# Weight tiles in pairs, and another form of the key and value loads, in a kernel of two attentions and two MoE layers on one core

## Chip, core and metric

One core of a Trainium2 chip. The metric is device time in microseconds (us) of one execution of the whole program, the median of several runs. Lower is better. The engines are named as the profile names them: PE (TensorE matmul; PEld its weight load), DVE (VectorE), ACT (ScalarE), POOL (GpSimd) and SP (SyncE, which issues all DMAs here).

## What is computed

The inputs q, k and v are float32 of shape (2, 8, 576, 64): two batches, eight heads, 576 tokens. The weights of the two layers come in float64.

```python
q_d, k_d, v_d = means of q, k, v over groups of 4 tokens   # 144 rows
out_up    = repeat(softmax(q_d @ k_d.T / 8) @ v_d, 4)
out_local = softmax(where(|i - j| < 4, q @ k.T / 8, -1e9)) @ v
x = out_up + out_local          # seen as 1152 tokens x 512

h = x @ w_in                    # 512 -> 2048
g = (a0 + a1*h + a2*h*h + a3*h*h*h) / (1 + |b0|*|h| + |b1|*h*h + 1e-6)
x = g @ w_out                   # 2048 -> 512

h = x @ w_in2
out = (h * tanh(softplus(h))) @ w_out2
```

## The kernel before

**Planner.** The kernel is first written as some thousand tasks (`add`, line 79), each with the engines that may run it and an estimated duration, a priority (a due time in us), the tasks it waits for, and the buffers it takes or uses. `Plan.run` (line 105) then plays the program through with these durations and writes every engine's instructions in the order in which they start there. The order within an engine is fixed from then on; on the chip an instruction waits on semaphores for what it needs, and all that stand behind it on its engine wait too. Where PE would idle for too long in the first part, `fill` (line 147) writes matmuls whose result nobody reads (lines 445 and 448), which keep its clock up; these are called fillers here.

**Attention.** Four pairs of heads in each of two batches are worked in 24 units (`unit`, line 532) of up to four windows of 64 queries. `prep` (line 469) does once per pair what its units share: it loads two heads of k with one DMA (96 partitions, six tokens of two heads in each, so pieces of 64 words), turns them round with six PE transposes (line 467), copies them into kT in two passes of 288 words (line 492), sums groups of four (line 500), and loads v for the down-sampled attention with one DMA over 72 partitions (line 509) that lines 518 and 522 sum. A unit loads its queries (line 546) and two windows of v (line 558), makes the scores (lines 612 to 623), the softmax (ACT line 640, DVE lines 633 to 666, POOL line 660), transposes (678, 682), the two products with v (713, 719), and writes x as two float32 parts, xh and xl (749, 754).

**MoE.** All products are made in three matmuls from a high and a low part of each operand. The 2048 columns of a layer are taken in groups (6, 6 and 4 tiles of 128 in the first layer, four times 4 in the second), and in each group the tokens in chunks: 256, 256, 256 and 384 in the first group of the first layer, else three times 384. A step is two tiles of one chunk: h by line 974, the rational function (ACT 995, 1000, 1003; DVE 1010, 1013, 1018 and others) or Mish (1068), its high and low part, and the second product by line 1122 or 1124. Steps with 384 tokens use buffers and banks of the attention, so they wait for its end (`att_done`, line 825), and so do the weights of all groups but the first (`gate`, line 842).

**Weights.** Each of the 64 weight tiles of 128 x 512 words comes as 64-bit words by one DMA into one of four raw buffers (line 848 for w_in, 853 for w_out) and is made into two float32 parts without 64-bit arithmetic: ACT scales the upper words (859) and shifts the lower ones (865), DVE joins them (872) and sets the sign (878), ACT or DVE writes the high part (884, 886), DVE the low part (889). Four buffers `wt` hold what is between; the parts go to rings of six tiles for each of w_in and w_out, after attention of nine.

```python
raw_t = [const.tile([128, DM], w_in1.dtype, name=f"raw{i}") for i in range(NRAW)]
wt_t = [const.tile([128, DM], F32, name=f"wt{i}") for i in range(NWT)]
x = add({"sp": 1.45}, load, pr - LLEAD, take=[r], chain="wld")
y = add({"act": 0.52}, scale, c, after=[x], take=[t], use=[r], chain="wsc")
z = add({"act": 0.52}, low, c, after=[x], use=[r])
x = add({"dve": t_dve(DM)}, join, c, after=[y, z], use=[t, r], port=True)
x = add({"dve": t_dve(DM)}, sign, c, after=[x], use=[t, r], port=True)
```

**What sets the order.** A step's due time is the PE time of all steps before it. Attention units of a chunk are due LEAD before it, the load of a weight tile LLEAD and its conversion CLEAD before its first step, w_out tiles OLAG after w_in; VOFF, VROFF, LOFF and KOFF shift the loads of attention (lines 26 to 36).

## Time and profile before

| what | value |
|---|---|
| median of 3 runs | 522.7 us (521.2 to 527.63) |
| the profiled execution | 523.05 us, of which its span 521.3 us |
| granted TensorE clock, mean | 0.993 |
| PE busy | 500.3 us, 96% of the span, 3530 matmuls |
| DVE busy | 378.4 us, 73%, 648 instructions |
| ACT busy | 356.1 us, 68%, 734 instructions |
| POOL busy | 74.2 us, 14%, 102 instructions |
| DMA | 46.54 MB, mean 89 GB/s, 56764 packets, 32784 of them under 512 B |

The span runs from the first instruction to the last. Busy time counts an engine's instructions, fillers as well; a busy PE is not PE at its peak. The shares are averages over stages with different limits.

### The profile page before, as it was taken

Reading aid. Unit: us, or ns where it says so; the run is one execution under the profiler, and the core shown is the slowest. Engines: PE = TensorE matmul, PEld = TensorE weight load, DVE = VectorE, ACT = ScalarE, POOL = GpSimd, SP = SyncE. Lnnn points to the kernel's source line nnn. Section 1 sums busy time; section 2 is a strip of 40 time slices with the busy share of each in tenths; the row PEclk is TensorE's granted clock in tenths of the full one; section 3 lists DMA queues with packets and bytes.
Section 4 is the critical chain, followed back from the end, with each engine's and each line's share of the span. In section 5 each row is a group of like instructions: output and inputs, shape, how many; then the busy total and the mean of one; then the engine's idle time right before and its main releaser. Section 6 shows DMA issues by size and latency. Waiting matters only on the chain.

```text
span 521.3 us, 9187 instructions
## 1 busy us (share of the span) xinstructions
PE 500.3 (96%) x3530; PEld 450.5 (86%) x3530; DVE 378.4 (73%) x648; ACT 356.1 (68%) x734; POOL 74.2 (14%) x102
## 2 busy tenths in 40 slices
PE   9889998988999999999799999999999999999997
PEld 5567676877999999999799989989998999889995
DVE  4777889898999999988999999998732632231322
ACT  4588788898788899998999998789821521112210
POOL 3553564234100000000000033400000000000000
PEclk9998999999999999999999999999999999999999
DMA  9979655432132114311340222467600000000111
GB/s 160 192 182 190 118 124 142 128 94 60 43 123 79 41 41 121 123 53 70 121 162 3 98 63 80 123 189 236 219 2 0 1 1 1 0 1 0 62 60 62
DMA packets 56764, 46.54 MB, mean 89 GB/s; under 512 B 32784, under 2 KB 51472, under 8 KB 56720
## 3 DMA queue, kind: packets, MB, share of 16 engines
q1 hardware_dynamic: 56720, 45.95, 33.2%
q8 instruction: 28, 0.46, 0.4%
q14 instruction: 16, 0.13, 0.1%
HBM read 43.58 MB, written 2.36 MB: 88 GB/s over the span
## 4 chain that ended last, share of the span: by engine, by line
PE 50%; ACT 20%; DVE 16%; DMA 8%; issue 3%; SPq 2%; POOL 0%; ACTq 0%; DVEq 0%
PE psum L974 22%; PE psum L1124 19%; PE psum L1122 5%; DMA raw<-in_moe_w_in_dram 3%; DMA raw<-in_moe_w_out_dram 2%; ACT wt L859 2%; ACT raw L865 2%; ACT wrk L1000 2%; ACT att L640 1%; ACT late_f L1003 1%; DMA wrk<-in_v_dram 1%; DVE part L1167 1%; ACT late_f L995 1%; ACT gg L1089 1%; DVE wt L878 1%
## 5 line engine op out<-in xcount | busy, mean ns | idle before, releaser
L974 PE MATMUL psum<-xh,wi 128*128 128x384 f32 (+1 forms) x600 | 153.4, 326 | 1.5 <-DVE wrk L1018 0.8
L974 PEld LDWEIGHTS psum<-xh,wi 128*128 128x128 f32 x600 | 107.1, 188 | 3.9 <-DVE wrk L1018 1.2
L974 PE MATMUL psum<-xl,wi 128*128 128x384 f32 (+1 forms) x300 | 96.5, 322 | 0.0
L1122 PE MATMUL psum<-gg,wo 128*128 128x256 f32 (+1 forms) x432 | 68.4, 311 | 1.3 <-DVE gg L1094 0.4
L1122 PEld LDWEIGHTS psum<-gg,wo 128*128 128x128 f32 x432 | 64.5, 189 | 3.4 <-DVE wo L889 0.8
L974 PE MATMUL psum<-xh,late_r 128*128 128x384 f32 x216 | 57.6, 335 | 0.7 <-DVE late_f L1018 0.7
L974 PEld LDWEIGHTS psum<-xl,wi 128*128 128x128 f32 x300 | 56.5, 188 | 0.3
L859 ACT ACTIVATE wt<-raw 128x512 f32<-128x512 f32 x64 | 43.0, 674 | 9.2 <-DVE wrk L1013 2.3
L1124 PE MATMUL psum<-wo,gg 128*128 128x512 f32 x207 | 48.8, 390 | 0.0
L872 DVE SCALAR_TENSOR_TENSOR wt<-wt,raw 128x512 int32<-128x512 int32 x64 | 44.8, 716 | 4.4 <-ACT raw L865 2.4
L1124 PEld LDWEIGHTS psum<-wo,gg 128*128 128x128 f32 x207 | 38.8, 188 | 7.9
L878 DVE SCALAR_TENSOR_TENSOR wt<-raw,wt 128x512 int32<-128x512 int32 x64 | 45.0, 711 | 0.2
L865 ACT ACTIVATE raw<-raw 128x512 int32<-128x512 uint16 x64 | 42.9, 676 | 2.8 <-DMA raw<-in_moe_w_out_dram 1.9
L1068 ACT ACTIVATE wrk<-psum 128x768 f32<-128x768 f32 (+1 forms) x13 | 10.2, 787 | 48.5 <-PE psum L974 48.5
L1201 DVE TENSOR_TENSOR part<-psum,part 128x512 f32<-128x512 f32 x27 | 18.2, 691 | 34.3 <-PE psum L1124 34.3
L1181 POOL TENSOR_TENSOR xl<-part,xh 128x768 fp32r<-128x768 f32 x6 | 14.3, 2396 | 184.3 <-DVE xh L1178 175.1
L974 PEld LDWEIGHTS psum<-xh,late_r 128*128 128x128 f32 x216 | 39.3, 188 | 1.2 <-PE psum L974 1.0
L1068 ACT ACTIVATE late_f<-psum 128x768 f32<-128x768 f32 (+1 forms) x12 | 9.4, 782 | 40.1 <-PE psum L974 40.1
L974 PE MATMUL psum<-xl,late_r 128*128 128x384 f32 x108 | 36.2, 336 | 0.0
L1094 DVE TENSOR_TENSOR gg<-wrk,gg 128x768 fp32r<-128x768 f32 (+2 forms) x23 | 19.4, 849 | 20.9 <-ACT gg L1068 20.8
L1094 DVE TENSOR_TENSOR gg<-late_f,gg 128x768 fp32r<-128x768 f32 x14 | 13.4, 956 | 18.9 <-ACT gg L1068 18.3
L448 PE MATMUL psum<-mask,ident 128*128 128x480 bf16 x89 | 24.0, 375 | 0.1
(133 smaller groups left out, 1010.1 us busy)
## 6 DMA issues: line engine op xcount, KB each, us to landing
raw<-in_moe_w_in_dram SPq DMA_DIRECT2D x32, 512.0 KB, 4.1
raw<-in_moe_w_out_dram SPq DMA_DIRECT2D x32, 512.0 KB, 6.3
out_dram<-part SPq DMA_DIRECT2D x9, 256.0 KB, 2.0
att<-in_v_dram SPq DMA_DIRECT2D x32, 60.0 KB, 4.3
att<-in_k_dram SPq DMA_DIRECT2D x6, 288.0 KB
att<-in_v_dram SPq DMA_DIRECT2D x6, 288.0 KB
att<-in_q_dram SPq DMA_DIRECT2D x16, 96.0 KB, 4.5
att<-in_v_dram SPq DMA_DIRECT2D x8, 80.0 KB, 7.9
```

The costliest lines, as they stand in the source:

```text
L448: nc.tensor.matmul(view[:, :6 * WK], ident16, mask[:, :6].rearrange("p w x -> p (w x)"), start=True, stop=True)
L859: nc.scalar.activation(out=t.v, in_=words(r)[:, :, 1].bitcast(F32), func=AF.Identity, scale=2.0 ** -112)
L865: nc.scalar.activation(out=words(r)[:, :, 0], in_=r.v.bitcast(U16).rearrange("p (n four) -> p n four", four=4)[:, :, 1], func=AF.Copy, sca ...
L872: nc.vector.scalar_tensor_tensor(out=ti, in0=ti, scalar=3, in1=words(r)[:, :, 0], op0=ALU.logical_shift_left, op1=ALU.bitwise_or)
L878: nc.vector.scalar_tensor_tensor(out=ti, in0=words(r)[:, :, 1], scalar=SIGN, in1=ti, op0=ALU.bitwise_and, op1=ALU.bitwise_or)
L974: nc.tensor.matmul(st.h.v[:, i, :T], w.v[:, ww, ks], xx[:, kk, c0:c0 + T], start=(nn == 0 and (st.big or i == 0)), stop=(nn == 3 * KD - 1 ...
L1068: nc.scalar.activation(out=vw(dst), in_=H(), func=AF.Mish)
L1094: ENG[e].tensor_tensor(out=vw(st.gl), in0=vw(st.c), in1=vw(st.gh).bitcast(F32), op=ALU.subtract)
L1122: nc.tensor.matmul(A(d)[:, :T], w.v[:, ww, sl], vw(gg)[:, i, :], start=start, stop=stop)
L1124: nc.tensor.matmul(A(d), vw(gg)[:, i, sl], w.v[:, ww, :], start=start, stop=stop)
L1181: ENG[e].tensor_tensor(out=xl[xs], in0=pv, in1=xh[xs].bitcast(F32), op=ALU.subtract)
L1201: nc.vector.tensor_tensor(out=pv, in0=acc.v[:, j], in1=pv, op=ALU.add)
```

## The change

Weight tiles are loaded and converted two at a time: a DMA of 128 x 1024 64-bit words, six passes of 1024 words instead of twice six of 512. Raw and `wt` buffers are two of double size instead of four, the rings three pairs for each kind, after attention five pairs for w_in and four for w_out. A step takes its half of a pair. In `prep`, the four pairs of heads that come first load each head's six tokens as one piece of 384 words, so a transpose holds two tokens of one head, and the copy to kT is four passes over 64 partitions instead of two over 128. The load of v is two DMAs, over 64 and over 8 partitions. Five numbers of the planner change, and some of its estimated durations.

```diff
-LEAD, CLEAD, LLEAD, OLAG = 30, 2, 35, 13
-PROL, PSTEP, VOFF, VROFF, LOFF, KOFF = -45, 1.5, 5, 0, 11, 12
+LEAD, CLEAD, LLEAD, OLAG = 25, 5, 35, 10
+PROL, PSTEP, VOFF, VROFF, LOFF, KOFF = -45, 1.5, 0, 0, 11, 12
...
-NRAW, NWT, NRING, NRING2 = 4, 4, 6, 3
+NRAW, NWT, NRING, NRING2 = 2, 2, 3, (2, 1)
...
-    raw_t = [const.tile([128, DM], w_in1.dtype, name=f"raw{i}") for i in range(NRAW)]
+    raw_t = [const.tile([128, 2 * DM], w_in1.dtype, name=f"raw{i}") for i in range(NRAW)]
...
+            if start:
+                nc.sync.dma_start(
+                    out=kn.v.rearrange("p (h x) -> p h x", h=2), in_=src.rearrange("h (p r) d -> p h (r d)", r=6)
+                )
...
+            if start:
+                for e2 in range(2):
+                    copies.append((
+                        lambda src=src, e2=e2: src()[64 * e2:64 * e2 + 64],
+                        lambda g=g, e2=e2: kT[p][64 * g:64 * g + 64].rearrange("c (p r e) -> c p r e", r=3, e=2)[:, :, :, e2],
+                        t, pt,
+                    ))
...
+            src = v[bb, 2 * p:2 * p + 2].rearrange("h (t p f) d -> p (h t) (f d)", t=2, f=4)
+            dst = vr.v.rearrange("p x f d -> p x (f d)")
+            for lo, hi in ((0, 64), (64, 72)):
+                nc.sync.dma_start(out=dst[lo:hi], in_=src[lo:hi])
...
-                    in_=src[:, f * 128:(f + 1) * 128].rearrange("(k p) f -> p k f", p=128),
+                    in_=src[:, f * 256:(f + 1) * 256].rearrange("(k p) f -> p k f", p=128),
...
-                nc.sync.dma_start(out=r.v, in_=(w_out1, w_out2)[m][f * 128:(f + 1) * 128, :])
+                nc.sync.dma_start(
+                    out=r.v.rearrange("p (a d) -> p a d", a=2),
+                    in_=(w_out1, w_out2)[m][f * 256:(f + 1) * 256, :].rearrange("(a p) d -> p a d", p=128),
+                )
...
-            y = add({"act": 0.52}, scale, c, after=[x], take=[t], use=[r], chain="wsc")
-            z = add({"act": 0.52}, low, c, after=[x], use=[r])
-            x = add({"dve": t_dve(DM)}, join, c, after=[y, z], use=[t, r], port=True)
+            y = add({"act": 1.04}, scale, c, after=[x], take=[t], use=[r], chain="wsc")
+            z = add({"act": 1.04}, low, c, after=[x], use=[r])
+            x = add({"dve": t_dve(2 * DM)}, join, c, after=[y, z], use=[t, r], port=True)
...
-                w, wd = W[m, "i", f]
+                w, wd = W[m, "i", f // 2]
```

The lines of the changed kernel that answer to those above: fillers 445 and 448 as before; key loads 475 (start) and 479, key copies 508 and 510, v load 530, windows of v 576, queries 564; weight loads 866 and 871, weight passes 880, 886, 893, 899, 905, 907 and 910; h product 996, second product 1144 and 1146; last attention product 737.

Three places in the order of the engines' instructions. First SP, at the start, from the fourth key load on (`in_k`, `in_q`, `in_v` are the inputs, `att` and `wrk` the memory that receives them). Before:

```order
L474 DMA wrk<-in_k_dram 96x12x64
L546 DMA att<-in_q_dram 128x4x64
L509 DMA att<-in_v_dram 72x4x256
L509 DMA wrk<-in_v_dram 72x4x256 x2
L546 DMA att<-in_q_dram 96x4x64
L558 DMA att<-in_v_dram 80x4x64 x2
L546 DMA att<-in_q_dram 64x4x64
L558 DMA att<-in_v_dram 80x4x64 x2
L509 DMA att<-in_v_dram 72x4x256
L546 DMA att<-in_q_dram 96x4x64
L558 DMA att<-in_v_dram 80x4x64 x2
L848 DMA raw_71<-in_moe_w_in_dram 128x4x128
```

Now, from the first load of v on:

```order
L530 DMA att<-in_v_dram 64x4x256
L530 DMA att<-in_v_dram 8x4x256
L576 DMA att<-in_v_dram 80x4x64 x2
L530 DMA wrk<-in_v_dram 64x4x256
L530 DMA wrk<-in_v_dram 8x4x256
L576 DMA att<-in_v_dram 80x4x64 x2
L530 DMA wrk<-in_v_dram 64x4x256
L530 DMA wrk<-in_v_dram 8x4x256
L530 DMA att<-in_v_dram 64x4x256
L530 DMA att<-in_v_dram 8x4x256
L564 DMA att<-in_q_dram 96x4x64
L866 DMA raw_71<-in_moe_w_in_dram 128x4x256
```

The loads of v and the first windows of v now stand ahead of the fifth query load, and one weight load of double size takes the place of the first two. Second ACT, where the first weight tiles are converted among the softmax passes (640, now 658) of attention. Before:

```order
L640 ACTIVATE att<-psum,att 128x80 x4
L644 ACTIVATE att<-psum,att 128x144
L859 ACTIVATE wt_75<-raw_71 128x512
L699 ACTIVATE att<-psum 80x512
L865 ACTIVATE raw_71<-raw_71 128x512
L859 ACTIVATE wt_76<-raw_72 128x512
L865 ACTIVATE raw_72<-raw_72 128x512
L731 ACTIVATE att<-psum 128x64
L640 ACTIVATE att<-psum,att 128x80 x3
```

Now:

```order
L605 ACTIVATE att<-psum 128x192
L880 ACTIVATE wt_73<-raw_71 128x1024
L658 ACTIVATE att<-psum,att 128x80 x4
L662 ACTIVATE att<-psum,att 128x144
L749 ACTIVATE att<-psum 128x64
L717 ACTIVATE att<-psum 80x512
L439 ACTIVATE b_sb<-b_sb 128x2
L605 ACTIVATE att<-psum 128x128
L767 ACTIVATE xh<-att 128x256
L886 ACTIVATE raw_71<-raw_71 128x1024
```

Four passes of 512 words have become two of 1024; the first of them now stands ahead of the softmax passes of a unit with four windows (658 x4), where before such passes stood ahead of it. Third PE at the last attention product (lines 713 and 719, now 731 and 737; `wi` and `wo` are weight tiles, `mask` with 480 columns a filler). Before:

```order
L448 LDWEIGHTS ident_62
L448 MATMUL psum<-mask,ident_62 128x480
L974 MATMUL psum<-xh,wi_79 128x256
L974 MATMUL psum<-xl,wi_79 128x256
L974 MATMUL psum<-xh,wi_79 128x256
L974 MATMUL psum<-xh,wi_80 128x256
L974 MATMUL psum<-xl,wi_80 128x256
L974 MATMUL psum<-xh,wi_80 128x256
L713 MATMUL psum<-att 64x48 x4
L719 MATMUL psum<-att 64x64 x6
L1122 MATMUL psum<-gg,wo_90 128x256 x12
L974 MATMUL psum<-xh,wi_79 128x256
```

Now:

```order
L1144 MATMUL psum<-gg,wo_80 128x256 x24
L696 MATMUL psum<-ident,att 72x128 x2
L700 MATMUL psum<-ident,att 80x128 x3
L996 MATMUL psum<-xh,wi_76 128x256
...
L731 MATMUL psum<-att 64x48 x4
L737 MATMUL psum<-att 64x64 x6
L996 MATMUL psum<-xh,wi_76 128x256
...
L1144 MATMUL psum<-gg,wo_78 128x256 x24
L996 MATMUL psum<-xh,wi_75 128x384
```

Fillers stand close to the last product before and not now; the MoE work on both sides of it is another part of the first group, and the first product of 384 columns comes sooner after it.

## Rows read from the trace of the kernel before

**Rows 1.** Busy time of each engine by stretches (us), granted clock, DMA share

```profile
core 0: us, PE busy (x) PEld busy (x) DVE busy (x) ACT busy (x) POOL busy (x), PEclk, DMA share, GB/s
0.00:140.00 140.00, 127.53 (x1489) 97.87 (x1490) 113.76 (x294) 110.62 (x386) 59.92 (x96) 0.99 0.63 134
140.00:310.00 170.00, 165.91 (x989) 163.48 (x987) 160.78 (x214) 156.88 (x213) 4.25 (x2) 0.99 0.27 84
310.00:521.00 211.00, 206.83 (x1055) 189.12 (x1054) 103.89 (x142) 88.58 (x136) 10.00 (x4) 1.00 0.20 64
...
100.00:120.00 20.00, 18.21 (x207) 15.14 (x206) 19.24 (x44) 19.40 (x58) 6.25 (x10) 1.00 0.34 99
```

**Rows 2.** Groups by form: fillers on PE; count, busy us, mean ns, idle before

```profile
L448 PE MATMUL psum<-mask,ident 128*128 128x480 bf16 x89 | 24.0, 375 | 0.1
L445 PE MATMUL psum<-part 128*128 128x480 bf16 x9 | 3.8, 604 | 1.2 <-DVE part L452 1.2
```

**Rows 3.** DMA queue from 0 to 20 us, then from 20 to 40 us

```profile
q1 hardware_dynamic: 9826, 3.19, 101.6%
...
q1 hardware_dynamic: 6889, 3.88, 79.0%
```

**Rows 4.** Timeline, waits for DMAs at the start: DVE, ACT, POOL

```profile
16.43 0.69 DVE L518 TENSOR_TENSOR wrk<-wrk 72x512 f32<-72x512 f32 x1 [0.78 <-DMA wrk<-in_v_dram]
...
27.29 0.68 ACT L859 ACTIVATE wt<-raw 128x512 f32<-128x512 f32 x1 [0.92 <-DMA raw<-in_moe_w_in_dram]
...
24.64 1.26 POOL L518 TENSOR_TENSOR att<-att 72x512 f32<-72x512 f32 x1 [3.80 <-DMA att<-in_v_dram]
```

**Rows 5.** Groups by form: a weight pass and MoE passes of two sizes

```profile
L872 DVE SCALAR_TENSOR_TENSOR wt<-wt,raw 128x512 int32<-128x512 int32 x64 | 44.8, 716 | 4.4 <-ACT raw L865 2.4 <-ACT wt L859 1.8
...
L1010 DVE TENSOR_TENSOR wrk<-wrk,psum 128x768 f32<-128x768 f32 x8 | 7.6, 952 | 3.4 <-ACT late_f L1003 1.6 <-ACT wrk L1000 1.5 <-ACT wrk L1003 0.3
L1013 DVE SCALAR_TENSOR_TENSOR wrk<-wrk,b_sb 128x512 f32<-128x512 f32 x9 | 7.1, 790 | 0.0
L1010 DVE TENSOR_TENSOR wrk<-wrk,psum 128x512 f32<-128x512 f32 x9 | 6.1, 682 | 1.4 <-ACT wrk L1003 1.3 <-ACT wrk L1000 0.2
...
L1000 ACT ACTIVATE wrk<-psum 128x768 f32<-128x768 f32 x18 | 14.5, 805 | 1.1 <-DVE wrk L1018 1.1
L1000 ACT ACTIVATE wrk<-psum 128x512 f32<-128x512 f32 x9 | 5.3, 593 | 0.0
```

**Rows 6.** Chain that ended last: start us, us, what

```profile
96.05 1.42 PE psum L974 x12
...
230.15 1.20 DVE wt L872 x2
```

**Rows 7.** Timeline of ACT: two weight passes in a row

```profile
41.94 0.68 ACT L859 ACTIVATE wt<-raw 128x512 f32<-128x512 f32 x1
42.50 0.67 ACT L865 ACTIVATE raw<-raw 128x512 int32<-128x512 uint16 x1
```

**Rows 8.** Timeline of PE at the fifth query flip, and fillers

```profile
18.60 0.36 PE L467 MATMUL psum<-ident,att 96*128 96x96 f32 x2 [0.86 <-DVE att L666]
18.79 0.97 PE L448 MATMUL psum<-mask,ident 128*128 128x480 bf16 x4
```

**Rows 9.** Timeline of ACT: two key copies of the start

```profile
9.41 0.80 ACT L492 ACTIVATE att<-psum 128x288 f32<-128x288 f32 x2 [2.03 <-PE psum L467]
```

**Rows 10.** Timeline of SP: the issue of the fifth query load

```profile
10.28 0.62 SPq L546 DMA_DIRECT2D att<-in_q_dram  x1
```

**Rows 11.** Timeline of PE: last attention product; both products of a 384-column step

```profile
132.53 0.53 PE L719 MATMUL psum<-att 80*64 80x64 f32 x12
...
160.27 0.34 PE L974 MATMUL psum<-xh,wi 128*128 128x384 f32 x1
...
176.72 4.32 PE L1122 MATMUL psum<-late_r,wo 128*128 128x384 f32 x24
```

More of the change, by code (lines that the diff above doesn't have):

```diff
@@ L473, in load @@
             src = k[bb, 2 * p:2 * p + 2]
-            nc.sync.dma_start(
-                out=kn.v.rearrange("p (r h d) -> p r h d", h=2, d=D),
-                in_=src.rearrange("h (p r) d -> p r h d", r=6),
-            )
-        ld = add({"sp": 1.6}, load, prio - KOFF, take=[kn], chain="ld")
+            if start:
+                nc.sync.dma_start(
+                    out=kn.v.rearrange("p (h x) -> p h x", h=2), in_=src.rearrange("h (p r) d -> p h (r d)", r=6)
+                )
+            else:
+                nc.sync.dma_start(
+                    out=kn.v.rearrange("p (r h d) -> p r h d", h=2, d=D),
+                    in_=src.rearrange("h (p r) d -> p r h d", r=6),
+                )
+        ld = add({"sp": 0.9 if start else 1.6}, load, prio - KOFF, take=[kn], chain="ld")
         copies = []
@@ L549, in qload @@
             )
-        l0 = add({"sp": 0.7}, qload, prio - LOFF, take=[qn], chain="ld")
+        l0 = add({"sp": 0.18 * nw}, qload, prio - LOFF, take=[qn], chain="ld")
         s0, step, m0 = window(w0, nw)
@@ L839 @@
         gate = []
-        if not (m == 0 and f < GROUPS[0][0]):
+        if not (m == 0 and 2 * f < GROUPS[0][0]):
             w.slots = ring_s[kind] + ring2[kind]
@@ L889, in lo @@
             ENG[e].tensor_tensor(out=w.v[:, 1], in0=s.v, in1=w.v[:, 0].bitcast(F32), op=ALU.subtract)
-        x = add({"sp": 1.45}, load, pr - LLEAD, take=[r], chain="wld")
+        x = add({"sp": 2.9}, load, pr - LLEAD, take=[r], chain="wld")
         src = r
```

55 lines of the change are left out of this document (29 added, 26 removed).

## Prediction

> **What bounds the kernel now.** I read the busy table by stretches first [rows 1]. Its TensorE (PE) column is the room that is left: from 310 us on PE is busy 206.8 of 211 us at full clock, from 140 to 310 it is busy 165.9 of 170. These 381 us are PE work and can give back little: 4.1 us idle in the middle, and some 1.7 us for a granted clock of 0.99 there (170 x 0.01). The first 140 us are another matter. PE is "busy" for 127.5 us, but the groups by form [rows 2] show that 3.8 + 24.0 = 27.8 us of it are 9 + 89 matmuls of lines 445 and 448, the fillers that the planner sets where it expects PE to idle. With 12.5 us of plain idle PE loses 40 us of these 140, while VectorE (DVE) is busy for 113.8 and ScalarE (ACT) for 110.6 us. So the change has to earn its time before 140 us, where attention, MoE steps and weight conversion share ACT and DVE. Last I read the DMA rows of the first 40 us, 16 engines taken by 101.6% and 79% [rows 3], and who waited for a DMA there [rows 4].
>
> **The passes.** In the order of instructions DVE has 205 weight passes before (64 x 3 and 13 casts) and 107 now; ACT has 179 before and 85 now. A merged pass saves its fixed part. DVE takes 952 ns for 768 words and 682 for 512 [rows 5]: 1.05 ns a word, 0.54 us for 512. Two passes of 512 back to back take 1.20 us in the chain [rows 6], 0.60 each, so 0.06 is fixed. ACT takes 805 and 593 ns [rows 5]: 0.83 ns a word, 0.43 us for 512. A pass of line 865 starts 0.56 us after one of line 859 [rows 7], so 0.13 is fixed. In all that is 98 x 0.06 = 5.9 us of DVE and 94 x 0.13 = 12.2 us of ACT, spread over the 64 tiles; it reaches the end only where PE waits for them.
>
> The Trainium skill, page "Perfetto Trace Analysis", section "Optimizing Scalar/DVE Operations", gives about 60 ns of overhead for a DVE and 93 ns for a ScalarE instruction on SBUF. The trace agrees for DVE and shows more for ACT; by the page ACT would save 94 x 0.093 = 8.7 us, an estimate.
>
> **What is moved ahead of the last attention step.** I count the order of both programs up to the last attention product (line 719 before, 737 now). Ahead of it stand 98 fillers before and 82 now, and 150 + 60 MoE matmuls of 256 columns before and 186 + 144 now. The 120 more are 120 x 1.42/12 [rows 6] = 14.2 us of PE work done earlier. DVE pays for it: up to the last attention add it has 14 more MoE passes (48 for 34) of some 0.74 us, the middle of 0.68 and 0.79 [rows 5], = 10.4 us; its weight passes go from 37 x 0.72 = 26.6 to 22 x (0.72 + 0.54) = 27.7 us. If DVE paces attention, attention ends 11.5 us later with 14.2 us more done: a gain of 2.7. If ACT paces it: 13 more MoE passes x 0.59 = 7.7, weight passes from 42 x 0.68 = 28.6 to 23 x (0.68 + 0.43) = 25.5, 8 more key copies at 0.40 (two take 0.80 [rows 9]) = 3.2; that is 7.8 us more, a gain of 6.4. By fillers: 16 fewer, between 0.20 us each where they follow one another (four in 0.97 us, the last shown with its whole 0.375 [rows 2, 8]) and 27.8/98 = 0.28: 3.2 to 4.5. I take 2.9, between DVE and the fillers at their pace, since DVE is as busy as ACT or busier; the ends are 2.7 and 6.4.
>
> **The start.** Four key loads go from 1152 pieces of 256 B each to 192 of 1536 B: 3840 packets fewer for the same bytes. From 0 to 20 us a packet of 325 B costs 1.016 x 16 x 20 us/9826 = 33 ns, from 20 to 40 us one of 563 B costs 37 [rows 3]. Along that line 256 B cost 32 and 1536 B 51 ns, and the engines are free (4608 x 32 - 768 x 51)/16 = 6.8 us earlier; if bytes alone set the price, it is 0. What waits for DMAs now: DVE 0.78 us for a value load, ACT 0.92 for a weight tile, POOL 3.80 for a value load [rows 4]. DVE's and ACT's, 1.7 us, lie on the path; with half of POOL's it is 3.6, with all of it 5.5, the upper end. Against it stand the 8 key copies on ACT (3.2 us), of which the 2.03 us that ACT idles beside them [rows 9] hide most, and on SP the fifth query load, now behind 12 value DMAs instead of 3. Nine issues of about 0.62 us put it at 10.28 + 5.6 = 15.9 us [rows 10]; its flip ran at 18.60, after a wait for DVE [rows 8], so a load that takes over 2.7 us to land is late on PE. One wait is added: on ACT the first weight pass (line 880) now stands ahead of the fourth unit's softmax, before (859) it stood behind it and still waited at 27.29 [rows 4]. Its load, of double size, follows the query load on SP, at some 16.5 us; if it lands 8 us later, the softmax and all that ACT does for the next units stand behind a wait of up to 3.5 us. I take a gain of 1.5; the ends are 5.5 and a loss of 3.2 + 3.5 = 6.7.
>
> **The middle.** PE's 5.8 us of idle and slow clock between 140 and 310 lie behind ACT and DVE, both busy for over 92% there [rows 1]. With some per cent less load I take half of it, 2.9, between 0 and 5.8. Against it: the first step of 384 columns now has 48 matmuls of 384 at 4.32/24 and 48 of 256 between its own two products, 8.6 + 5.7 = 14.3 us; before, 16.3 us lay between them (160.4 to 176.7 [rows 11]) with ACT and DVE full. 2.0 us may be missing; the net is 0.9. The two raw buffers of double size and the rings of 10 and 8 tiles (9 and 9 before) I cost at nothing: 16 tiles are issued by the end of attention in both orders, and the last pair of the second group's output weights has over 20 us of PE work between the release of its buffer and its use. If that cover goes, the three DVE passes of a pair (3 x 1.14 us) show once a group. Two of the six 768-word differences on POOL go to DVE at the switch to the second MoE, 2 x 0.95 us beside PE's own work.
>
> The sum is 2.9 + 1.5 + 0.9 = 5.3 us. The profiled execution took 523.05 us (span 521.3), 0.35 above the median of 522.7; it becomes 517.75, the median 517.4.
>
> **The rivals.** (A) It is hidden: the DMA waits of the start turn into waits for the key copies, the later query load and line 880, and DVE takes the lead of 14.2 us back. For it: by count 11.5 of the 14.2 are taken back already. Against it: 16 fillers fewer. Time 522.7, within 2. (B) ACT paces attention and the start gives all it has: 6.4 + 5.5 + 2.9 - 2.0 = 12.8, time 509.9. For it: ACT at 19.4 of 20 us from 100 to 120 us; against it DVE at 19.2 in the same row [rows 1]. (C) The cover is missing. The MoE work now done before attention ends is what PE lived on after it, while the first 384-column step went through ACT and DVE and while the second group's weights, which wait for attention to end, were converted. Before, 222 matmuls of 256 columns were left after the last attention product, 26.3 us; now it is 102, 12.1 us, against a latency of 16.3. If the whole lead is given back as idle there, the time is 517.4 + 14.2 = 531.6; slower than before from 5.3 us of new idle on. (D) Long passes block: a step behind a weight pass waits up to 1.14 instead of 0.60 us on DVE and 0.99 instead of 0.56 on ACT. There are 192 of these passes; each puts on average half the difference, 0.24 us, on what stands behind it. If one in four of these waits reaches PE, that is 192 x 0.24/4 = 11.5 us, time 528.9; it decides from about one in nine. For it: ACT and DVE have gaps in attention, where single steps wait for each other; against it: from 140 us on PE rarely waits at all.
>
> The same section of the Trainium skill says that where these engines are not saturated but cause bubbles elsewhere, breaking instructions up may let work finish sooner, the rule behind (D). The trace shows them saturated from 100 us on and not in the first 60.
>
> **How the numbers follow.** The forecast (513 to 521) has 0.43, A 0.18, B 0.19, C 0.11, D 0.09. Two per cent, about what a measurement of this kernel can tell from no change, is 512.2 to 533.2. Faster than that is B and a little of the forecast, 0.21; slower the upper parts of C and D, 0.07; within it 0.72. The range of 508 to 530 leaves out the far ends of B, C and D.
>
> **What would show it.** Right: passes near 1.2 us on DVE and 1.1 on ACT in the groups; fillers and idle of PE together under 36 us up to 140; the last attention product near 142 us (132.5 [rows 11] + 14.2 - 2.9 - 1.5), between 138 and 148; PE idle from there to 310 under 8 us. Wrong: over 6 us of PE idle in one place after attention (C); PE or ACT waiting often behind lines 893, 899 or 880 (D); ACT waiting over 2 us before line 880, or late with the key copies (A); attention's end before 138 (B).

## The result, and the profile after

| | before | after |
|---|---|---|
| median of 20 runs | 524.41 us (521.2 to 531.16) | 519.12 us (515.97 to 522.71) |
| ratio, 95% interval | | 0.9907 (0.9882 to 0.9932) |
| the profiled execution | 523.05 us, span 521.3 | 521.48 us, span 519.7 |
| granted TensorE clock in it, mean | 0.993 | 0.993 |

The change takes 0.93% off, 4.9 us of 524.41 by the ratio, and the interval lies wholly below 1. The forecast was 1.0%, 5.3 us, and 517.4 us lies 1.7 us below the median. Read the two profiles with care: they differ by only 1.6 us, because the profiled execution of before lies 1.4 us below the median of its kernel and that of after 2.4 us above.

First the busy time of after by stretches, to be laid beside [rows 1].

```profile
core 0: us, PE busy (x) PEld busy (x) DVE busy (x) ACT busy (x) POOL busy (x), PEclk, DMA share, GB/s
0.00:140.00 140.00, 124.77 (x1472) 97.62 (x1473) 114.00 (x273) 110.86 (x367) 60.75 (x95) 0.98 0.59 133
80.00:100.00 20.00, 17.97 (x179) 14.14 (x181) 16.20 (x33) 15.34 (x50) 5.68 (x7) 0.83 0.43 130
140.00:310.00 170.00, 165.30 (x997) 161.28 (x997) 159.44 (x178) 155.82 (x186) 3.81 (x4) 1.00 0.26 87
310.00:520.00 210.00, 205.78 (x1049) 187.99 (x1047) 100.06 (x102) 79.28 (x97) 8.01 (x3) 1.00 0.18 62
```

From 310 us on nothing has changed: all PE, at full clock. Before that PE has 15.2 us of idle in the first 140 us (12.5 before), and in 80 to 100 us its clock is at 0.83, a third of that stretch at the lower of its two levels, worth 20 x 0.17 = 3.4 us. DVE and ACT are as full as before. Next the fillers of after by form, against [rows 2].

```profile
L448 PE MATMUL psum<-mask,ident 128*128 128x480 bf16 x74 | 20.4, 390 | 0.0
L445 PE MATMUL psum<-part 128*128 128x480 bf16 x8 | 3.3, 566 | 1.2 <-DVE part L452 1.2
```

They take 23.7 us instead of 27.8. So in this execution 4.1 us came from fillers and 2.7 went into idle. Third, the weight passes of after by form, against [rows 5].

```profile
L899 DVE SCALAR_TENSOR_TENSOR wt<-raw,wt 128x1024 int32<-128x1024 int32 x32 | 39.1, 1222 | 0.4
L893 DVE SCALAR_TENSOR_TENSOR wt<-wt,raw 128x1024 int32<-128x1024 int32 x32 | 38.9, 1219 | 3.8 <-ACT raw L886 2.8 <-ACT wt L880 0.8
L886 ACT ACTIVATE raw<-raw 128x1024 int32<-128x1024 uint16 x32 | 37.0, 1156 | 2.6 <-DMA raw<-in_moe_w_in_dram 2.2 <-DMA raw<-in_moe_w_out_dram 0.4
L880 ACT ACTIVATE wt<-raw 128x1024 f32<-128x1024 f32 x32 | 36.7, 1149 | 17.0 <-DMA raw<-in_moe_w_out_dram 9.7 <-DMA raw<-in_moe_w_in_dram 5.9 <-DVE late_r L910 1.1
```

Line 893 is line 872 of before: 38.9 us for 44.8. The last row holds a cost that before hardly had: ahead of line 880 ACT idles 15.6 us in all for weight loads (9.7 + 5.9), where it was 3.1 ahead of line 859, of them 7.8 in the first 140 us, as its waits there show (total, times, longest).

```profile
ACT wt L880 <- DMA raw<-in_moe_w_out_dram: 5.5, 2, 3.9
...
ACT wt L880 <- DMA raw<-in_moe_w_in_dram: 2.3, 4, 1.2
```

The longest can be followed in the chain of waits (start, us, what): with two raw buffers a load starts when DVE has done with the pair before it, and among attention's loads this one takes 8.10 us to land.

```profile
68.58 1.15 DVE wt L899
69.73 0.02 SPq L871
...
69.78 8.10 DMA raw<-in_moe_w_out_dram
```

The timeline of ACT has the wait at its end (in brackets), and that of the first pair, which the prediction feared, at 24.22 us.

```profile
24.22 1.16 ACT L880 ACTIVATE wt<-raw 128x1024 f32<-128x1024 f32 x1 [0.49 <-DMA raw<-in_moe_w_in_dram]
...
77.98 1.14 ACT L880 ACTIVATE wt<-raw 128x1024 f32<-128x1024 f32 x1 [3.90 <-DMA raw<-in_moe_w_out_dram]
```

The wait goes on to PE. An attention copy of ACT (line 749) stands behind the two weight passes, DVE waits for it and PE for DVE. The last two rows are busy times again, with the clock in the third column from the right.

```profile
80.24 0.36 DVE L756 TENSOR_TENSOR att<-psum,att 128x192 f32<-128x192 f32 x1 [2.06 <-ACT att L749]
...
80.92 0.39 PE L467 MATMUL psum<-ident,att 96*128 96x96 f32 x2 [1.72 <-DVE att L712]
```

```profile
79.00:82.40 3.40, 1.19 (x20) 0.75 (x20) 2.16 (x4) 3.40 (x14) 0.56 (x1) 1.00 0.02 5
82.40:89.20 6.80, 6.24 (x38) 3.67 (x36) 4.97 (x11) 3.59 (x10) 2.25 (x3) 0.50 0.62 190
```

From 79.0 to 82.4 us PE is busy for 1.19 of 3.40 us, and then its clock stands at the lower level for 6.8 us: 2.2 us of idle and 3.4 us of clock at this one place. It is no accident of one execution. Of the experiments below, six keep the changed kernel's order, and with it that makes seven profiles: in each ACT's wait of 2.7 to 4.3 us ends 0.1 us after this same load lands, 6.9 to 8.5 us after its issue (in two of them the profile names a DVE pass that ended within the same 0.1 us), and from between 79 and 85 us on the clock is at the lower level for 6.8 us. The kernel before has two such falls, half as long, at 47 and 259 us. No run has a third raw buffer, so what it would give back is open.

On PE's timeline the last attention product stands at 146.31 (132.53 before [rows 11]). Behind it no wait is longer than 0.92 us; PE's waits from there to 335 us are all for the high and low parts of g.

```profile
146.31 0.56 PE L737 MATMUL psum<-att 80*64 80x64 f32 x12
```

```profile
PE psum L1144 <- ACT gg L1111: 1.7, 3, 0.9
PE psum L1144 <- DVE gg L1116: 1.7, 4, 0.6
PE psum L1144 <- DVE late_r L1116: 0.4, 1, 0.4
PE psum L1144 <- ACT late_r L1111: 0.3, 1, 0.3
```

**How the experiments are read.** The granted clock of one kernel differs from execution to execution (0.977 to 1.000 in those of the kernel before), and the time with it. So each kernel has two numbers: the ratio of its runs to those of the kernel before on the same chip, and a mean "at full clock", in which (1 - granted clock) x span is taken off each run. At full clock the kernel before stands at 519.9, 519.8, 519.5 and 519.1 us in the four sets of runs, after at 515.6, so small differences are better seen there; the standard errors are 0.2 to 0.8 us. Executions over 1.5% above the fastest of their kernel are left out of the ratio, the clock and this mean, but not of the median.

Three limits of this. The changed kernel itself was run for the result and in none of these four sets, so every difference to it goes across sets, and differences under 1 us are not told from nothing. The full loss is taken off, while over the executions of one kernel the time follows the loss by 0.8 of it; with 0.8 the differences used below change by 0.3 us or less, those of the two kernels with the lowest clocks (0.984 and 0.987) by 1.1 and 0.6. And a lower clock that an edit itself brings about is taken off too, as the 3.4 us at 82 us are; the ratio keeps it.

| kernel | median us | ratio (95%) | clock | at full clock |
|---|---|---|---|---|
| after | 519.12 | 0.9907 (0.9882 to 0.9932) | 0.992 | 515.6 |
| key and value part alone | 532.22 | 1.0128 (1.0068 to 1.0189) | 0.991 | 527.3 |
| planner numbers alone | 528.57 | 1.0078 (1.0041 to 1.0116) | 0.991 | 523.6 |
| pairs alone | 531.18 | 1.0111 (1.0046 to 1.0176) | 0.989 | 525.4 |
| keys, values and numbers | 541.97 | 1.0353 (1.0306 to 1.0399) | 0.984 | 533.2 |
| pairs, keys and values | 528.62 | 1.0079 (1.0041 to 1.0116) | 0.987 | 521.4 |
| pairs and numbers | 525.07 | 0.9982 (0.9936 to 1.0029) | 0.990 | 519.2 |
| after, passes halved | 525.84 | 1.0018 (0.9982 to 1.0053) | 0.993 | 520.4 |
| after, ACT's passes halved | 523.51 | 1.0015 (0.9988 to 1.0042) | 0.990 | 518.2 |
| after, DVE's passes halved | 523.14 | 1.0015 (0.9986 to 1.0044) | 0.993 | 518.9 |
| after, keys in 256 B pieces | 519.41 | 0.9918 (0.9889 to 0.9947) | 0.993 | 515.9 |
| after, values in one DMA | 521.33 | 0.9985 (0.9960 to 1.0010) | 0.991 | 516.5 |
| after, both loads as before | 520.59 | 0.9943 (0.9910 to 0.9976) | 0.992 | 516.8 |

### The profile page after: what moved, and what is told of

Read it like the earlier page. It is cut to its first block, busy times and chain, and to the rows that moved or that the text cites. A ratio compares the mean times of both kernels' runs of the same rounds, so it can differ in the third digit from the quotient of the medians.

```text
span 519.7 us, 8875 instructions
## 1 busy us (share of the span) xinstructions
PE 495.9 (95%) x3514; PEld 446.9 (86%) x3514; DVE 373.5 (72%) x551; ACT 346.0 (67%) x647; POOL 72.6 (14%) x102
## 4 chain that ended last, share of the span: by engine, by line
PE 53%; DVE 15%; ACT 13%; DMA 6%; issue 3%; ACTq 0%; DVEq 0%; SPq 0%
PE psum L996 23%; PE psum L1146 19%; PE psum L1144 7%; DMA raw<-in_moe_w_in_dram 5%; DVE wt L899 2%; DVE wt L893 2%; DMA raw<-in_moe_w_out_dram 2%; DVE wrk L1032 1%; ACT wrk L1022 1%; ACT late_f L1025 1%; ACT wrk L1017 1%; ACT wt L880 1%; DVE late_f L1032 1%; ACT att L658 1%; ACT raw L886 1%
## 5 line engine op out<-in xcount | busy, mean ns | idle before, releaser
L996 PE MATMUL psum<-xh,wi 128*128 128x384 f32 (+1 forms) x528 | 132.0, 324 | 0.0
L1144 PE MATMUL psum<-gg,wo 128*128 128x384 f32 (+1 forms) x456 | 73.7, 314 | 3.8 <-ACT gg L1111 1.7
L996 PE MATMUL psum<-xh,late_r 128*128 128x384 f32 x288 | 76.1, 335 | 0.0
L880 ACT ACTIVATE wt<-raw 128x1024 f32<-128x1024 f32 x32 | 36.7, 1149 | 17.0 <-DMA raw<-in_moe_w_out_dram 9.7
L893 DVE SCALAR_TENSOR_TENSOR wt<-wt,raw 128x1024 int32<-128x1024 int32 x32 | 38.9, 1219 | 3.8 <-ACT raw L886 2.8
L899 DVE SCALAR_TENSOR_TENSOR wt<-raw,wt 128x1024 int32<-128x1024 int32 x32 | 39.1, 1222 | 0.4
L886 ACT ACTIVATE raw<-raw 128x1024 int32<-128x1024 uint16 x32 | 37.0, 1156 | 2.6 <-DMA raw<-in_moe_w_in_dram 2.2
L1116 DVE TENSOR_TENSOR gg<-wrk,gg 128x768 fp32r<-128x768 f32 (+1 forms) x22 | 18.5, 842 | 23.0 <-ACT gg L1090 22.2
L996 PEld LDWEIGHTS psum<-xl,late_r 128*128 128x128 f32 x144 | 27.0, 188 | 0.3
L1146 PE MATMUL psum<-wo,late_r 128*128 128x512 f32 x108 | 25.6, 391 | 0.0
```

What stands on the lines that cost most here:

```text
L880: nc.scalar.activation(out=t.v, in_=words(r)[:, :, 1].bitcast(F32), func=AF.Identity, scale=2.0 ** -112)
L886: nc.scalar.activation(out=words(r)[:, :, 0], in_=r.v.bitcast(U16).rearrange("p (n four) -> p n four", four=4)[:, :, 1], func=AF.Copy, sca ...
L893: nc.vector.scalar_tensor_tensor(out=ti, in0=ti, scalar=3, in1=words(r)[:, :, 0], op0=ALU.logical_shift_left, op1=ALU.bitwise_or)
L899: nc.vector.scalar_tensor_tensor(out=ti, in0=words(r)[:, :, 1], scalar=SIGN, in1=ti, op0=ALU.bitwise_and, op1=ALU.bitwise_or)
L996: nc.tensor.matmul(st.h.v[:, i, :T], w.v[:, ww, ks], xx[:, kk, c0:c0 + T], start=(nn == 0 and (st.big or i == 0)), stop=(nn == 3 * KD - 1 ...
L1116: ENG[e].tensor_tensor(out=vw(st.gl), in0=vw(st.c), in1=vw(st.gh).bitcast(F32), op=ALU.subtract)
```

## Experiments: the parts of the change, alone and in twos

The change has three parts: pairs of weight tiles, the key and value loads and copies, and four planner numbers (LEAD, CLEAD, OLAG and VOFF; "five" in the section on the change is one too many). The first set tries each alone, and the pairs with the numbers.

**Key and value part alone.**

```diff
+            if start:
+                nc.sync.dma_start(
+                    out=kn.v.rearrange("p (h x) -> p h x", h=2), in_=src.rearrange("h (p r) d -> p h (r d)", r=6)
+                )
...
+            for lo, hi in ((0, 64), (64, 72)):
+                nc.sync.dma_start(out=dst[lo:hi], in_=src[lo:hi])
```

The edit also has the half copies of the keys, takes one dependency of these copies away (`t_cd`), and changes the planner's estimates for the copies and for the issue of the key, value and query loads, which can move the order by themselves.

> The kernel before with only the key and value loads and copies of the change (and the two estimates of their issue). Measured for the whole change: 0.9907 of before, 4.9 us. Theory of the prediction (the gain is moved work plus start plus middle): only the start's term, 1.5 us less, ratio 0.997; its fillers go from 98 to 106, so a little less is possible. Theory that the whole gain is the start (loads and copies): ratio 0.991, 518 to 520 us. Theory that the key copies cost more than the packets save: 1.00 to 1.01.

Measured 1.0128, 7.4 us slower at full clock. None of the three theories had that much.

**Planner numbers alone.**

```diff
-LEAD, CLEAD, LLEAD, OLAG = 30, 2, 35, 13
-PROL, PSTEP, VOFF, VROFF, LOFF, KOFF = -45, 1.5, 5, 0, 11, 12
+LEAD, CLEAD, LLEAD, OLAG = 25, 5, 35, 10
+PROL, PSTEP, VOFF, VROFF, LOFF, KOFF = -45, 1.5, 0, 0, 11, 12
```

> The kernel before with only the four planner numbers of the change (lead 25, conversion lead 5, output lag 10, value offset 0). 102 MoE matmuls more (12.1 us of PE) then stand ahead of the last attention product, and the weight passes stay single. Prediction: DVE pays for what is moved (MoE passes and weight passes earlier), so the time stays within 0.3%: 0.997 to 1.003. Theory that the order alone gives the gain: 0.991. Theory that order without cheaper passes is harmful: over 1.004.

Measured 1.0078: harmful without cheaper passes, as the third theory had it. Moving 12.1 us of PE work ahead of attention's end is no gain by itself.

**Pairs alone.**

```diff
-NRAW, NWT, NRING, NRING2 = 4, 4, 6, 3
+NRAW, NWT, NRING, NRING2 = 2, 2, 3, (2, 1)
...
+                    in_=src[:, f * 256:(f + 1) * 256].rearrange("(k p) f -> p k f", p=128),
```

> The changed kernel without its key and value part and with the planner numbers of before: pairs alone. 33 MoE matmuls more than before stand ahead of the last attention product (3.9 us), 4 fillers more in all. Prediction: pass savings of 5.9 us on DVE and 12.2 on ACT are worth 1 to 2 us: ratio 0.996 to 0.998. Theory that the passes alone bring the gain: 0.991. Theory that long passes and loads block what stands behind them, and that the new numbers were needed to make up for it: 1.004 or more.

Measured 1.0111. The pairs need the numbers.

**Pairs and numbers, keys and values as before.**

```diff
-            for lo, hi in ((0, 64), (64, 72)):
-                nc.sync.dma_start(out=dst[lo:hi], in_=src[lo:hi])
+            nc.sync.dma_start(
+                out=vr.v.rearrange("p x f d -> p x (f d)"),
+                in_=v[bb, 2 * p:2 * p + 2].rearrange("h (t p f) d -> p (h t) (f d)", t=2, f=4),
+            )
```

> The changed kernel with key and value loads and copies as before (pairs of weight tiles and the new planner numbers stay). Prediction: moved work 2.9 and middle 0.9 stay, 3.8 us less than before, ratio 0.993. Theory that the whole gain is the start: 1.000. Theory that it is all passes and numbers: 0.991 or a little less.

Measured 0.9982 (0.9936 to 1.0029), 519.2 at full clock: 0.7 us of gain, where 3.8 were expected. So every part alone loses, these two together about break even, and all three gain. The other two pairings complete the picture.

**Key and value part with the numbers.** The edit is the first two diffs together.

> The kernel before with the key and value part and the four planner numbers of the change, weight tiles still single. Alone the key and value part measured 1.0128 and the numbers 1.0078. If effects add up: 1.021. If the new numbers are what makes the key and value part useful (the changed kernel against the one without that part: 0.9907 / 0.9982 = 0.9925): 1.0078 x 0.9925 = 1.000. If only all three parts together fit: over 1.01.

Measured 1.0353, worse than the sum of both. **Pairs with the key and value part, numbers as before:**

```diff
-LEAD, CLEAD, LLEAD, OLAG = 25, 5, 35, 10
-PROL, PSTEP, VOFF, VROFF, LOFF, KOFF = -45, 1.5, 0, 0, 11, 12
+LEAD, CLEAD, LLEAD, OLAG = 30, 2, 35, 13
+PROL, PSTEP, VOFF, VROFF, LOFF, KOFF = -45, 1.5, 5, 0, 11, 12
```

> The changed kernel with the four planner numbers of before. Pairs alone measured 1.0111, key and value part alone 1.0128. If effects add up: 1.024. If the numbers are a tuning to the two other parts, worth what they are worth to the pairs alone (0.9982 / 1.0111 = 0.987): 0.9907 / 0.987 = 1.004. Prediction's reading (moved work 2.9 us, as the numbers move 87 more matmuls ahead of the last attention product here than without them): 0.996.

Measured 1.0079, 521.4 at full clock: less than the sum of the two alone. The same edit, the four numbers, is worth -5.8 us at full clock on top of pairs and keys (521.4 to 515.6) and +3.7 on its own.

**Where these kernels lose.** PE's time divides up: its own work is the same in all, the rest is idle time, fillers and clock. The table is worked out from each trace: gaps between PE's matmuls up to the last attention product, gaps from there until MoE matmuls worth 200 us at full clock are done (at 315 to 334 us), and fillers. What follows that mark takes PE 200.1 to 201.9 us in every one.

```
                           idle to attention's end   idle from there to the mark   fillers
before                               12.2                       4.9                    98
after                                15.4                       4.5                    82
keys and values alone                12.6                       9.1                   106
numbers alone                        10.2                       9.2                    96
pairs alone                          13.6                      10.1                   102
keys, values, numbers                12.8                      17.4                   103
pairs, keys and values               11.5                       8.9                    98
pairs and numbers                    11.2                       6.5                    95
```

All five that are slower than before lose in the middle column, 4 to 12.5 us. The worst of them shows how; these are PE's longest waits in it between 140 and 335 us.

```profile
PE psum L992 <- ACT late_f L1021: 5.1, 1, 5.1
PE psum L992 <- ACT wrk L1021: 5.0, 1, 5.0
...
PE psum L992 <- DVE late_f L1036: 2.2, 1, 2.2
```

Lines 1013, 1018 and 1021 of that kernel are the three passes of ACT that read h from PSUM, the memory that PE writes its products to (995, 1000 and 1003 before); DVE reads it twice beside them, and after the last read the next h may be written to the same place, a bank of PSUM. Its ACT timeline around one of these waits:

```profile
282.62 0.98 ACT L1013 ACTIVATE late_f<-psum,a_sb 128x768 f32<-128x768 f32 x1
283.62 1.28 ACT L935 ACT_TABLE_LOAD   x1
284.91 0.94 ACT L946 ACTIVATE wrk<-wrk,bias 128x768 f32<-128x768 f32 x1
285.75 0.92 ACT L946 ACTIVATE late_f<-late_f,bias 128x768 f32<-128x768 f32 x1
286.58 0.79 ACT L1018 ACTIVATE wrk<-psum 128x768 f32<-128x768 f32 x1
287.38 1.28 ACT L935 ACT_TABLE_LOAD   x1
288.68 0.84 ACT L951 ACTIVATE wrk<-wrk 128x768 f32<-128x768 f32 x1
289.43 0.83 ACT L951 ACTIVATE late_f<-late_f 128x768 f32<-128x768 f32 x1
290.16 0.88 ACT L1021 ACTIVATE late_f<-psum,b_sb 128x768 f32<-128x768 f32 x1
```

And PE behind it, on its timeline:

```profile
291.09 0.69 PE L992 MATMUL psum<-xh,wi 128*128 128x384 f32 x1 [5.05 <-ACT late_f L1021]
```

ACT is never idle in these 8.4 us, and still PE stands for 5.05: between the first and the last read of one h (282.62 to 290.16) the order has put two table loads with two passes each of other steps. In the changed kernel the same three reads stand close together behind such a block:

```profile
218.27 1.58 ACT L954 ACTIVATE late_f<-late_f 128x768 f32<-128x768 f32 x2
219.76 0.98 ACT L1017 ACTIVATE wrk<-psum,a_sb 128x768 f32<-128x768 f32 x1
220.63 0.80 ACT L1022 ACTIVATE wrk<-psum 128x768 f32<-128x768 f32 x1
221.32 0.84 ACT L1111 ACTIVATE gg<-late_f 128x768 fp32r<-128x768 f32 x1
222.06 0.84 ACT L1111 ACTIVATE late_r<-wrk 128x768 fp32r<-128x768 f32 x1
222.79 0.90 ACT L1025 ACTIVATE wrk<-psum,b_sb 128x768 f32<-128x768 f32 x1
```

From the first to the start of the last it is 3.0 us instead of 7.5. A table load (ACT_TABLE_LOAD, 1.28 us in these rows) stands ahead of passes with another function. All kernels have the same 17 behind attention; which reads they fall between is an outcome of the planner's list, which any edit throws about. Pairs with keys and values, the mildest of the five at full clock, has two waits of the kind too:

```profile
PE psum L996 <- DVE late_f L1040: 3.6, 2, 2.3
PE psum L996 <- ACT late_f L1025: 3.0, 1, 3.0
```

The waits of the h products for such reads, by ACT or DVE, add up to 13.7 us in the worst between 140 and 335 us, to 7.6 for the pairs alone, 6.6 for pairs with keys and values, 5.3 for pairs and numbers and 4.9 for keys and values alone; to 0.7 before and to none after. The numbers alone are another case: 1.7 us of this kind, and 7.5 of waits for the parts of g.

The same traces can be divided at attention's end. Times are at full clock here (multiplied by the granted clock of the stretch). The third column is the MoE work that stands ahead of that end and did not before, at 0.118 us a matmul. The gain ahead is this work less the time by which attention ends later; the gain behind is the time by which the rest is shorter, less this work.

```
                          end of attention   from there on   moved   gain ahead   gain behind
before                         131.4             386.5
after                          143.5             372.6        14.2       2.1         -0.3
keys and values alone          133.7             391.4         0.7      -1.6         -5.6
numbers alone                  140.4             378.7        12.1       3.1         -4.3
pairs alone                    135.3             387.7         3.9      -0.1         -5.1
keys, values, numbers          141.8             387.2        12.4       2.0        -13.1
pairs, keys and values         132.5             385.9         3.9       2.8         -3.3
pairs and numbers              139.4             376.2        11.4       3.3         -1.1
```

The slower five lose behind attention, up to 13.1 us. The changed kernel loses next to nothing there, so what it gains it gains ahead. These are single executions; the first column differs by up to 3 us between traces of one order, the second by 0.4, as the second set shows.

So a kernel in which the order moves says little about the part that was edited. The second set of experiments leaves the order of the changed kernel alone.

## Experiments: one cost at a time, in the changed kernel's order

**All weight passes halved.** The same for the six kinds of pass:

```diff
-            nc.scalar.activation(
-                out=t.v, in_=words(r)[:, :, 1].bitcast(F32), func=AF.Identity, scale=2.0 ** -112
-            )
+            for h in HALVES:
+                nc.scalar.activation(
+                    out=t.v[:, h], in_=words(r)[:, h, 1].bitcast(F32), func=AF.Identity, scale=2.0 ** -112
+                )
...
+HALVES = (slice(0, 512), slice(512, 1024))
```

> The changed kernel with every pass over a pair of weight tiles written as two of 512 words, one behind the other, all else in the same order on every engine, the same loads. Prediction: it adds back the fixed parts, 0.06 us a pass on DVE and 0.13 on ACT, 1.4 us of DVE and 2.8 of ACT before attention ends and as much again up to 310 us: 2 to 4 us more than the changed kernel, ratio to before 0.994 to 0.998. Theory that the gain is the order and the loads and the fixed parts are hidden: within 0.8 us of the changed kernel, 0.990 to 0.992.

Measured 1.0018: more than both theories. At full clock it is 520.4 against 515.6, 4.8 us. The groups of this kernel by form:

```profile
L904 DVE SCALAR_TENSOR_TENSOR wt<-raw,wt 128x512 int32<-128x512 int32 x64 | 44.0, 728 | 0.0
L897 DVE SCALAR_TENSOR_TENSOR wt<-wt,raw 128x512 int32<-128x512 int32 x64 | 41.4, 690 | 1.6 <-ACT raw L889 1.6
L889 ACT ACTIVATE raw<-raw 128x512 int32<-128x512 uint16 x64 | 39.8, 682 | 3.1 <-DMA raw<-in_moe_w_in_dram 2.1 <-DMA raw<-in_moe_w_out_dram 0.9
L882 ACT ACTIVATE wt<-raw 128x512 f32<-128x512 f32 x64 | 39.6, 672 | 14.3 <-DMA raw<-in_moe_w_in_dram 6.1 <-DMA raw<-in_moe_w_out_dram 4.8 <-DVE att L596 3.0
```

These four kinds are 164.8 us of busy time here and 151.7 in the changed kernel. From start to start where passes follow one another without a gap (medians), DVE takes 1.135 us for 1024 words and 602 ns for 512, ACT 1.043 us and, in the kernel before, 568 ns: fixed parts of 69 and 93 ns. The 93 ns are a median over two kinds of pass, 103 for line 880 and 77 for 886, from few pairs each.

In this order the gain hangs on the merged pass: halve it and the time is that of the kernel before. Where it is lost the traces show. Behind attention's end the changed kernel takes 372.6 us at full clock, and the three kernels below that only change loads 372.5, 372.7 and 372.9; with all passes halved it is 375.8, with ACT's alone 374.4, with DVE's alone 375.1. So some 3.2 of the 4.8 us are lost behind attention. Ahead of it the seven traces of this order end attention between 140.7 and 143.6 us, halved or not, which leaves the rest of the 4.8 unseen in them.

**Only ACT's, only DVE's passes halved.**

```diff
-            for h in HALVES:
+            for h in WHOLE:
                 nc.vector.scalar_tensor_tensor(
...
+WHOLE = (slice(0, 1024),)
```

> The changed kernel with only ACT's weight passes written as two of 512 words, all else in the same order. With the passes of both engines split the time was 1.0018 of before, against 0.9907. ACT runs 85 weight passes; a split one costs 2 x 568 - 1043 = 93 ns more, 7.9 us in all. If ACT paces (rival B of the prediction): most of the 1.1% comes back, 0.999 to 1.002. If DVE paces (the prediction's choice): 0.991 to 0.994. If both add what they cost: about half, 0.996.

> The changed kernel with only DVE's weight passes written as two of 512 words. DVE runs 107; a split one costs 2 x 602 - 1135 = 69 ns more, 7.4 us in all. If DVE paces: 0.999 to 1.002. If ACT paces: 0.991 to 0.994. If both add what they cost: about half, 0.996.

The ratios are 1.0015 and 1.0015, and taken by themselves each would bring it all back, which can't be, as both together give no more. In that set the kernel before had a granted clock of 0.994 and these two 0.990 and 0.993. At full clock they are 518.2 and 518.9: 2.6 and 3.3 us above the changed kernel, together 5.9 for the 4.8 of both at once. That is the third theory: both add, 2.6 of 7.9 us on ACT and 3.3 of 7.4 on DVE. The changed kernel itself was not run in this set, so this rests on the correction by the clock, and on the traces behind attention: 1.8 and 2.5 us more there, 3.2 for both.

**Keys of the start in pieces of 256 B again.**

```diff
-                    out=kn.v.rearrange("p (h x) -> p h x", h=2), in_=src.rearrange("h (p r) d -> p h (r d)", r=6)
+                    out=kn.v.rearrange("p (r h d) -> p r h d", h=2, d=D),
+                    in_=src.rearrange("h (p r) d -> p r h d", r=6),
```

The half copies write to other places of kT accordingly.

> The changed kernel with the four key loads of the start in pieces of 256 B again, the same order on every engine (the half copies stay). Prediction: the packets are worth about 1.5 us: 520.6 us, ratio 0.9935. If the engines really give back 6.8 us earlier and weight loads pace attention (the changed kernel's ACT waits 7.8 us for weight tiles before 140 us): 3 to 6 us more, 0.996 to 1.002. If packets are hidden: 0.990 to 0.992.

Measured 0.9918, 0.3 us at full clock, not told from nothing: the packets are hidden. The DMA queue of the changed kernel from 0 to 20 us (packets, MB, share of 16 engines), and then of this one:

```profile
q1 hardware_dynamic: 5871, 3.32, 99.0%
```

```profile
q1 hardware_dynamic: 9618, 3.26, 105.6%
```

With 3747 packets more and nearly the same bytes the engines are taken by 6.6% more of 20 us, 1.3 us, where the price per packet from [rows 3] had given up to 6.8. The fourth key load lands at 12.00 us instead of 10.83.

**Each value load in one DMA again.**

```diff
-            for lo, hi in ((0, 64), (64, 72)):
+            for lo, hi in ((0, 72),):
```

> The changed kernel with each value load in one DMA of 72 partitions again, the same order on every engine. The key and value part is worth 0.9907 / 0.9982 beside the pairs and the numbers, and the packets of the keys next to nothing (0.9918 without them). If the split of the value loads carries it (POOL waits 3.8 us for a value load before the change, 2.7 after): 0.995 to 0.998. If what carries it is the order that the planner finds with it (82 fillers for 95): 0.990 to 0.992.

The ratio, 0.9985, lies just above the range of the split; at full clock it is 516.5 to 519.5 in this set, 0.994, between the two ranges, and 0.9 us above the changed kernel. The clock in its runs was 0.991 against 0.994 for the kernel before in this set. So the two readings differ, and **both loads as before** was to tell:

```diff
-            for lo, hi in ((0, 64), (64, 72)):
+            for lo, hi in ((0, 72),):
...
-                    out=kn.v.rearrange("p (h x) -> p h x", h=2), in_=src.rearrange("h (p r) d -> p h (r d)", r=6)
+                    out=kn.v.rearrange("p (r h d) -> p r h d", h=2, d=D),
+                    in_=src.rearrange("h (p r) d -> p r h d", r=6),
```

> The changed kernel with both loads of the key and value part as before (keys of the start in pieces of 256 B, each value load one DMA of 72 partitions), every engine's order and the half copies as in the changed kernel. The whole key and value part is worth 0.9907 / 0.9982 beside the pairs and the numbers; each load alone undone gave 0.9918 and 0.9985, at full clock 0.4 and 1.0 us. If the part works by the order that the planner finds with it: 0.990 to 0.995 (at full clock 515.5 to 517.5 us). If the two loads cover for each other and the part works by them: 0.997 to 1.000 (at full clock 519 us, as without the part).

Measured 0.9943 (0.9910 to 0.9976), 516.8 at full clock. Both lie in the order's range, though the interval of the ratio just reaches the other. The loads are worth 1.3 us, with a standard error of 0.3 and the step across sets on top. The key and value part as a whole is worth 3.6 beside the other two (519.2 to 515.6 at full clock), so 2.3 us of it come from the order that is found with it and from the half copies, which this kernel keeps; no run divides these two: 82 fillers for 95, at 27.8/98 = 0.28 us each 3.6 us of PE time, less what idle takes back.

## Why the prediction was right, and where its steps were not

**The bound and the total.** PE from 310 us on was read rightly, and so was the place where the time comes from, ahead of attention's end. 0.93% was measured, 1.0% forecast; at full clock 4.3 us of the 5.3.

**The passes.** Durations came out as said: 1219 and 1149 ns for "near 1.2" and "1.1". The fixed part on DVE was right (0.06 said, 0.069 measured). On ACT 0.13 was too large: it measured 0.093. The step that failed is the slope: 0.83 ns a word was taken from MoE passes that read PSUM, and lines 880 and 886 take (1043 - 568)/512 = 0.93. That PSUM makes the difference is not shown, as the casts of line 905 stay near 0.83 (521 ns for 512 words, some 950 for 1024). The figure of the Trainium skill that the prediction put beside it (page "Perfetto Trace Analysis", section "Optimizing Scalar/DVE Operations", 93 ns) was the right one. In all that is 98 x 0.069 + 94 x 0.093 = 15.5 us, and 4.8 of them reach the end, a little more than the whole gain. The prediction held that these savings only count where PE waits for them, and gave them no line of their own; they stand in its DVE count of what is moved and in the "less load" of the middle. It looked for the time before 140 us, and most of what halving costs is lost behind that: without the merged passes this order would give back 3.2 us there.

**What is moved.** The term of 2.9 counted 14.2 us of PE work done earlier against 11.5 us later. In the profiles attention ended 13.8 us later (132.53 to 146.31), 12.1 at full clock. So it is about 2 us in this pair, against the 4.4 of this term and the start's that had put attention's end near 142. But the profiled execution of after lies 2.3 us above the mean of its kernel at full clock (517.8 and 515.6), and behind attention its order takes the same in every trace; so the surplus lies ahead, and a mean execution gains about 4 there, an estimate. The size of the two terms together is not contradicted. And moving alone does not pay: the numbers alone move 12.1 us ahead and lose 3.7, as they give back behind attention what they gain ahead of it.

**The start.** 1.5 said, 1.3 measured for the loads, but not by packets: undone alone, those cost 0.3 and the divided value load 0.9, each under what these sets can tell. The feared wait for the first pair was 0.49 us and not up to 3.5. The half copies could not be told from the order.

**The buffers.** The prediction put the two raw buffers of double size at nothing, since as many tiles are issued by the end of attention. What it left out is when: the load that waits for one of the two lands late at 77.88 us, and PE loses 5.6 us behind it, 2.2 of idle and 3.4 of clock.

**The middle.** 0.9 said, next to nothing found: what is left behind attention takes 13.9 us less, and 14.2 us of work were moved out of it. Idle from attention's end to the mark went from 4.9 to 4.5, and the clock of that stretch from 0.99 to 1.00. The 2.0 us that might have been missing between the two products of the first 384-column step were not: the second one starts at 173.38 us without a wait.

**The rivals.** (A) Its sign appeared, ACT waiting 3.90 us before line 880, and fillers and idle up to 140 us came to 23.7 + 15.2 = 38.9 us, not under 36. It has the price of the buffers above, but did not decide: the median is lower all the same. (B) was half right: ACT paces too, 2.6 us against DVE's 3.3, but its sign, attention's end before 138 us, and its time did not come. (C) did not come: no wait after attention is over 0.92 us. (D) is not borne out, as halving costs time; passes with other work between the halves were not tried.

**What was not seen.** The prediction took the three parts as terms of a sum. They are not: at full clock 7.4 + 3.7 + 5.5 us of loss alone make 4.3 us of gain together. That the sum came out right rests on counts from the orders of the two whole programs, which hold the outcome of the planner's list already, and in part on luck: the buffers and the middle were each put too well, and the changed order happens to have none of the waits for PSUM reads that the others have. For the keys and values alone the same working said 1.5 us of gain, and 7.4 of loss were measured; for pairs and numbers it said 3.8, and 0.7 were measured.

## What to carry to other kernels

Where a planner orders the instructions, an edit acts twice, by its own cost and by the order that comes out; measure its own cost with the order held fixed, and read the order of the whole program, not of the part, for the rest: fillers, work ahead of a gate, and above all what stands between the reads that free a PSUM bank. Merging passes on the two engines that feed a full PE paid about a third to a half of the fixed parts saved on each. Compare medians, and of profiles only what is larger than two executions of one order differ by: here up to 3 us ahead of attention's end, but 0.4 us behind it, so there a single trace can tell 2 us.

## What the runs showed that was not expected

- A kernel whose ACT is busy without a gap can still hold PE for 5.05 us: what counts is where in ACT's order the last read of a bank stands.
- The price of small DMA pieces: 3747 more packets, with key pieces of 256 B instead of 1536 B, for nearly the same bytes took the 16 engines 1.3 us more of the first 20 us, and cost the program 0.3 us, not told from nothing.
- The granted clock of one and the same kernel ran from 0.977 to 1.000 between executions, and the time followed it, by 0.8 of the loss: 521.8 us at 1.000 and 529.6 at 0.977 among those of the kernel before.
- The two halves of a weight pass on ACT and on DVE cost 93 and 69 ns more than the whole (medians).
- One late load of a weight pair cost PE more by the fall of the clock that came behind the idle time (3.4 us) than by the idle time itself (2.2 us).
